# A second buffer for the high and low parts, taken from DMA scratch memory, the running logits sum on GpSimd, and new emission times

## The chip, the cores and the metric

The kernel runs on one core of one Trainium2 chip. The metric is device time in microseconds (us). The time before is the median of three runs, 523.21 us (522.85 to 523.69). One more execution was taken by the hardware profiler, and every duration in this document comes from it or from later profiles of the same kind.

Engine names follow the profile: PE is TensorE, PEld its weight loads, DVE is VectorE, ACT is ScalarE, POOL is GpSimd, SP is SyncE, whose queue issues most DMA transfers. L295 is line 295 of the kernel file.

## The reference

The reference computes attention over 4 batches, 8 heads, 768 positions and head size 64, in which a query sees only the keys whose 6-bit hash is the same as its own. The output feeds a soft mixture of experts.

```python
q_bits = (einsum(q, proj) > 0); k_bits = (einsum(k, proj) > 0)   # 6 bits each -> buckets
mask = q_bucket[:, :, :, None] == k_bucket[:, :, None, :]
scores = where(mask, scale * q @ k.T, -1e9)
attn = softmax(scores); x = attn @ v                      # then (4*768, 512)
logits = x @ phi                                          # 32 slots
d = softmax(logits, axis=0); slot_input = d.T @ x
slot_out[e] = relu(slot_input[e] @ w1[e]) @ w2[e]         # 8 experts, 4 slots each
out = softmax(logits, axis=1) @ slot_out
```

## The kernel before

There are 32 heads (4 batches of 8) and they are processed in pairs. For each pair one load brings `raw` (q and k of both heads, 2 x 128 x 768 floats). Because the fast matmul format of the kernel keeps fewer digits, q and k are split in a high and a low part: `split_hi` casts `raw` on ACT into parts 0 and 2 of the tile `w4` (L289, two casts), and `split_lo` writes raw minus high into parts 1 and 3 on DVE (L295, two operations; on POOL at L298 for the first pairs). `bits` makes the hash bits with eight matmuls (L332) and one DVE operation (`bt`, L325). Four kinds of DMA then spread rows of `w4` and `bt` over the operand tiles `XY` of each head: `spread_y`, `spread_l`, `spread_x`, `spread_bits`, all through line L302. `XY` has three buffers, `raw`, `w4` and `bt` one each.

For one head, `smax` (L375) multiplies into two PSUM buffers `smx`, and DVE takes row maxima of them (L378 and L381, nine reductions a head). `shift` turns the maxima into a row that `shift_rows` (L397 on PE, L400 on ACT, a DMA of `mr`) puts into `XY`. `scores` (L413) multiplies into three PSUM buffers `st`, and ACT takes the exponential into `pt` (L417). POOL adds the six blocks of `pt` into `acc` in five additions (L424 once, L430 four times), and `av` (L441, 24 matmul records) multiplies `pt` with `v`. `smax` of one head is interleaved with `scores` of the head before.

For a finished pair, `pair_sum`, `pair_turn` and `pair_rec` (L453, L489, L460) make reciprocals of the sums, `pair_x` (L504, L506) stores x, `pair_log` (L468) and `pair_add` make the pair's share of the logits: L480 multiplies, and L482 adds to the running sum `lacc` on DVE (not for the first pair of a batch). `batch_*` steps fold a batch into the slot softmax. After the last head the experts' layers run, with weights that `load_weights` has brought in during the attention.

The order of all this is written out by hand: each step has an emission time in the table `STEADY`, in slots relative to its pair (a pair is 12 slots, six a head), or in `ONCE`, in absolute slots. The steps are sorted by that time and emitted; an engine takes its instructions in exactly that order, and waits where the next one is not ready. The times only set the order; no step waits for a clock.

Of the kernel before, what the change touches and what calls it, by code (L numbers as in the profile page):

```python
# [42 lines left out]


STEADY = {
    ('acc', 0, 0): 0.91143595, ('acc', 0, 1): 3.17478349, ('acc', 0, 2): 3.59676867, ('acc', 1, 0): 10.88626624,
    ('acc', 1, 1): 11.33964379, ('acc', 1, 2): 11.82064114, ('av', 0, 0): 4.078226, ('av', 0, 1): 4.27318607,
    ('av', 0, 2): 4.47578804, ('av', 1, 0): 11.29101187, ('av', 1, 1): 11.30451101, ('av', 1, 2): 11.80872392,
    ('batch_both',): 20.1, ('batch_exp',): 23.0, ('batch_max',): 22.4, ('batch_scale',): 24.396,
    ('batch_share',): 27.6, ('batch_slots',): 26.173, ('batch_turn',): 23.9, ('batch_weigh',): 24.65,  # L50
    ('bits', 0): -13.95890534, ('load', 0): -21.84228255, ('load_v', 0): -1.51318162, ('load_v', 1): 4.63191299,
    ('pair_add', 0): 15.99028816, ('pair_log', 0): 15.89036858, ('pair_rec', 0, 0): 15.31234319,
    ('pair_rec', 0, 1): 15.74808174, ('pair_rec', 0, 2): 15.83774187, ('pair_sum', 0): 14.25462034,
    ('pair_turn', 0): 14.78228382, ('pair_x', 0, (0, 1)): 21.81002444, ('pair_x', 0, (2,)): 16.53595504,
    ('scores', 0, 0, 0): 0.42937858, ('scores', 0, 0, 1): 0.10975419, ('scores', 0, 1, 0): 0.37566801,
    ('scores', 0, 1, 1): 0.06354472, ('scores', 0, 2, 0): 2.73608952, ('scores', 0, 2, 1): 0.39545741,
    ('scores', 0, 3, 0): 1.17190303, ('scores', 0, 3, 1): 2.96375079, ('scores', 0, 4, 0): 0.91043595,
    ('scores', 0, 4, 1): 1.58215641, ('scores', 0, 5, 0): 2.32865234, ('scores', 0, 5, 1): 2.43752751,
    ('scores', 1, 0, 0): 6.82167698, ('scores', 1, 0, 1): 5.28419876, ('scores', 1, 1, 0): 5.49659969,
    ('scores', 1, 1, 1): 5.70056921, ('scores', 1, 2, 0): 9.5088345, ('scores', 1, 2, 1): 6.24519176,  # L60
    ('scores', 1, 3, 0): 6.27277748, ('scores', 1, 3, 1): 9.83928317, ('scores', 1, 4, 0): 9.71651955,
    ('scores', 1, 4, 1): 7.80253627, ('scores', 1, 5, 0): 9.44600188, ('scores', 1, 5, 1): 7.50325885,
    ('shift', 0): -2.89738435, ('shift', 1): 2.67478786, ('shift_rows', 0): -2.14833088,
    ('shift_rows', 1): 3.02147361, ('smax', 0, 0, 0): -7.00077299, ('smax', 0, 0, 1): -8.63468468,
    ('smax', 0, 1, 0): -8.20918051, ('smax', 0, 1, 1): -6.29379503, ('smax', 0, 2, 0): -5.39311908,
    ('smax', 0, 2, 1): -6.75745749, ('smax', 0, 3, 0): -6.47510133, ('smax', 0, 3, 1): -4.73315438,
    ('smax', 0, 4, 0): -8.59086819, ('smax', 0, 4, 1): -4.27385444, ('smax', 0, 5, 0): -4.25336427,
    ('smax', 0, 5, 1): -3.26636443, ('smax', 1, 0, 0): 2.40118286, ('smax', 1, 0, 1): -2.02963968,
    ('smax', 1, 1, 0): -2.01736929, ('smax', 1, 1, 1): 0.30153939, ('smax', 1, 2, 0): 0.03611274,
    ('smax', 1, 2, 1): 1.34851447, ('smax', 1, 3, 0): 1.74922724, ('smax', 1, 3, 1): 2.09633042,  # L70
    ('smax', 1, 4, 0): 2.28076515, ('smax', 1, 4, 1): -2.41700748, ('smax', 1, 5, 0): -2.06779907,
    ('smax', 1, 5, 1): 0.84522444, ('split_hi', 0): -14.12691859, ('split_lo', 0, 0): -13.3249754,
    ('split_lo', 0, 1): -13.04048452, ('spread_bits', 0): -13.92314133, ('spread_bits', 1): -8.21018051,
    ('spread_l', 0): -4.89960371, ('spread_l', 1): -6.85974162, ('spread_x', 0): -10.40239078,
    ('spread_x', 1): -7.05038, ('spread_y', 0): -11.52688803, ('spread_y', 1): -8.46779598,
}

ONCE = {
# [17 lines left out]
    ('one_turn', 31): 193.725, ('one_x', 30): 191.23, ('one_x', 31): 193.725, ('smax', 1, 0, 0): -2.3,  # L96
    ('smax', 1, 0, 1): -2.29, ('smax', 1, 1, 0): -2.28, ('smax', 1, 1, 1): -2.1, ('smax', 1, 2, 0): -2.05,
    ('smax', 1, 2, 1): -2.0, ('smax', 1, 3, 0): -1.99, ('smax', 1, 3, 1): -1.9, ('smax', 1, 4, 0): -1.8,
    ('smax', 1, 4, 1): 0.62, ('smax', 1, 5, 0): 0.63, ('smax', 1, 5, 1): 1.2, ('split_hi', 2): -1.5,
    ('split_lo', 2, 0): -1.45, ('split_lo', 2, 1): -1.44, ('spread_bits', 1): -7.869, ('spread_bits', 2): 0.4,  # L100
    ('spread_l', 0): -12.047, ('spread_l', 1): -12.02, ('spread_l', 2): 0.5, ('spread_x', 0): -12.04,
    ('spread_x', 1): -12.03, ('spread_x', 2): 0.6, ('spread_y', 1): -14.012, ('spread_y', 2): -1.2,
}


# [32 lines left out]
def lsh_attention_soft_moe(  # L138
# [141 lines left out]


    def split_hi(h):
        w = pp.tile([P, 4, S], F32R, name="w4", bufs=1)
# [4 lines left out]
        for x in range(2):
            nc.scalar.copy(w[:, 2 * x], st[h]["raw"][:, x])  # L289

    def split_lo(h, x):
        w = st[h]["w4"]
        raw = st[h]["raw"][:, x]
        if h > 2:
            nc.vector.scalar_tensor_tensor(out=w[:, 2 * x + 1], in0=raw, scalar=1.0, in1=w[:, 2 * x],  # L295
                                           op0=ALU.mult, op1=ALU.subtract)
# [175 lines left out]
    def pair_add(h):  # L472
        b, g = h // H, (h % H) // 2
        pt = st[h]["lp"]
        if g == 0:
# [4 lines left out]
        nc.vector.tensor_tensor(out=dst, in0=pt[:, 0:HC], in1=st[h]["rs"], op=ALU.mult)  # L480
        if g:
            nc.vector.scalar_tensor_tensor(out=lacc_of[b], in0=dst, scalar=1.0, in1=lacc_of[b],  # L482
                                           op0=ALU.mult, op1=ALU.add)
# [520 lines left out]
```

## Time and profile before

| | |
|---|---|
| median of three runs | 523.21 us |
| the profiled execution's own time | 524.37 us |
| its span, first to last instruction | 522.6 us |
| mean granted TensorE clock | 0.973 |
| PE busy | 482.3 us (92%) |
| DVE busy | 396.8 us (76%) |
| ACT busy | 245.6 us (47%) |
| POOL busy | 331.8 us (63%) |
| moved by DMA | 99.60 MB, mean 191 GB/s |

The span splits in a start (to about 31 us), the further pairs of heads, of some 27 us each, and the end (from about 452 us) with the experts' layers. Matmuls are pipelined, so busy time of PE is counted while any matmul is in flight; a gap of PE in the profile means that none was.

### The profile page before, as it was taken

To read this page: it belongs to the slowest core of one execution; us is meant where nothing else is said; L and a number is where in the kernel's file an instruction comes from. 1 tells how busy PE (TensorE), PEld (TensorE's weight loads), DVE (VectorE), ACT (ScalarE), POOL (GpSimd) and SP (SyncE) were. 2 spreads that over 40 slices of the span, in tenths; PEclk is the share of its full clock that TensorE was granted. 3 is DMA by queue.
4 is the path that set the end of the run, shared out by engine and by line. 5 is a ranking of instruction groups with operands and counts; after the bars stand their busy time and mean duration, and the time that the engine had idled before them with its cause. 6 is when DMAs were issued, how large, how long until landed. Compare 5 with 4: busy or idle time off the path is not lost.

```text
span 522.6 us, 9003 instructions
## 1 busy us (share of the span) xinstructions
PE 482.3 (92%) x3155; PEld 295.6 (57%) x3155; DVE 396.8 (76%) x700; ACT 245.6 (47%) x462; POOL 331.8 (63%) x226
## 2 busy tenths in 40 slices
PE   6889899999999999999999999999999999979992
PEld 4456565656565656565655656564656566453562
DVE  4735878989798989797998798989987967444333
ACT  4044546464555554545464636454745445412232
POOL 9258585868678776768587868586788687411200
PEclk9579999999999999999999999999999999989998
DMA  3757665666665557676656575757585676879977
GB/s 104 172 108 201 157 169 157 168 156 163 149 174 133 161 150 209 157 198 160 194 153 158 159 206 153 211 142 183 140 222 144 154 199 235 313 282 348 409 289 286
DMA packets 39802, 99.60 MB, mean 191 GB/s; under 512 B 7470, under 2 KB 13756, under 8 KB 39756
## 3 DMA queue, kind: packets, MB, share of 16 engines
q1 hardware_dynamic: 38956, 97.37, 64.9%
q10 hardware_dynamic: 608, 1.57, 1.4%
q8 instruction: 25, 0.41, 0.3%
q14 instruction: 21, 0.17, 0.1%
q0 software_dynamic: 192, 0.08, 0.1%
HBM read 52.76 MB, written 6.29 MB: 113 GB/s over the span
## 4 chain that ended last, share of the span: by engine, by line
PE 63%; DVE 14%; DMA 12%; SPq 5%; issue 3%; ACT 1%; DVEq 0%; ACTq 0%
PE st L413 17%; PE av L441 15%; PE smx L375 11%; DMA XY<-w 7%; DVE w L295 7%; SPq L302 5%; DMA XY<-bt 4%; PE qs L927 3%; PE qh L845 3%; PE av L243 2%; PE mi L468 2%; PE mi L453 2%; DVE mx L381 2%; PE mi L504 2%; DVE mx L378 2%
## 5 line engine op out<-in xcount | busy, mean ns | idle before, releaser
L430 POOL TENSOR_TENSOR acc<-acc,pt 128x768 f32<-128x768 f32 x125 | 239.8, 1919 | 72.0 <-ACT pt L417 64.5
L417 ACT ACTIVATE pt<-st 128x512 f32<-128x512 f32 x288 | 164.1, 597 | 66.3 <-PE st L413 55.9
L413 PE MATMUL st<-XY 128*128 128x512 f32 (+1 forms) x768 | 179.1, 347 | 2.3 <-DMA XY<-mr 2.3
L375 PE MATMUL smx<-XY 96*128 96x256 f32 (+1 forms) x384 | 127.4, 382 | 22.6 <-DVE mx L381 18.8
L381 DVE TENSOR_REDUCE mx<-smx 128x1 f32<-128x512 f32 x192 | 128.1, 680 | 15.8 <-PE smx L375 15.1
L413 PEld LDWEIGHTS st<-XY 128*128 128x128 f32 x768 | 127.7, 192 | 18.2 <-issue 4.2
L441 PE MATMUL av<-pt,v 128*64 128x384 f32 x768 | 130.9, 490 | 0.1
L375 PEld LDWEIGHTS smx<-XY 96*128 96x128 f32 x384 | 67.6, 194 | 59.5 <-DVE mx L381 30.4
L441 PEld LDWEIGHTS av<-pt,v 128*64 128x64 f32 x768 | 52.3, 137 | 76.0 <-issue 75.2
L424 POOL TENSOR_TENSOR acc<-pt 128x768 f32<-128x768 f32 x32 | 58.7, 1833 | 30.7 <-ACT pt L417 30.5
L295 DVE SCALAR_TENSOR_TENSOR w<-raw,w 128x768 fp32r<-128x768 f32 x28 | 60.3, 2192 | 22.8 <-ACT w L289 17.1
L378 DVE TENSOR_REDUCE mx<-smx 128x2 f32<-128x512 f32 x96 | 63.8, 678 | 13.2 <-PE smx L375 13.0
L445 ACT COPY avs<-av 128x384 f32<-128x384 f32 x32 | 15.3, 478 | 90.3 <-PE av L441 90.3
L289 ACT CAST w<-raw 128x768 fp32r<-128x768 f32 x32 | 25.0, 830 | 36.9 <-DMA XY<-w 14.8
L460 DVE RECIPROCAL sm<-sm 128x128 f32<-128x128 f32 x45 | 41.2, 919 | 0.0
L506 DVE TENSOR_TENSOR xq<-mi,r 128x256 f32<-128x256 f32 x45 | 17.6, 418 | 9.7 <-PE mi L504 9.7
L482 DVE SCALAR_TENSOR_TENSOR lacc<-sm,lacc 128x384 f32<-128x384 f32 x11 | 17.9, 1627 | 0.4
L504 PEld LDWEIGHTS mi<-ident,avs 128*128 128x128 f32 x90 | 10.4, 140 | 10.9 <-issue 9.0
L298 POOL TENSOR_TENSOR w<-raw,w 128x768 fp32r<-128x768 f32 x4 | 7.2, 1806 | 13.8 <-ACT w L289 13.8
L884 POOL CAST avs<-lacc 128x48 fp32r<-128x48 f32 x8 | 2.1, 265 | 21.5 <-ACT lacc L875 14.3
L504 PE MATMUL mi<-ident,avs 128*128 128x128 f32 x90 | 15.6, 282 | 0.0
L927 PE MATMUL qs<-w 128*32 128x256 f32 x232 | 15.2, 382 | 0.0
(169 smaller groups left out, 344.0 us busy)
## 6 DMA issues: line engine op xcount, KB each, us to landing
w<-w SPq DMA_DIRECT2D x61, 512.0 KB
XY<-w SPq DMA_DIRECT2D x61, 384.0 KB
raw<-qk SPq DMA_DIRECT2D x32, 384.0 KB
...
XY<-bt SPq DMA_DIRECT2D x62, 19.5 KB
```

Source lines behind the costliest of these rows:

```text
L295: nc.vector.scalar_tensor_tensor(out=w[:, 2 * x + 1], in0=raw, scalar=1.0, in1=w[:, 2 * x], op0=ALU.mult, op1=ALU.subtract)
L375: nc.tensor.matmul(pt[:, o:o + b - a], Ys[h % N_Y][0:96, 0, t * P:(t + 1) * P], Ys[h % N_Y][0:96, 1, a:b], start=True, stop=True)
L378: nc.vector.tensor_reduce(out=mx[:, n - 1:n + 1], in_=pt.rearrange("p (a x) -> p a x", a=2), axis=AX.X, op=ALU.max)
L381: nc.vector.reduce_max(out=mx[:, n:n + 1], in_=pt, axis=AX.X)
L413: nc.tensor.matmul(pt[:, o:o + b - a], x[:, 1, i * P:(i + 1) * P], x[:, 0, a:b], start=first, stop=not first)
L417: nc.scalar.activation(pts[i // 2][:, 512 * u:512 * u + 512], pt, AF.Exp, scale=D ** -0.5)
L424: nc.gpsimd.tensor_tensor(out=s["acc"], in0=pr[:, 0:S], in1=pr[:, S:2 * S], op=ALU.add)
L430: eng.tensor_tensor(out=s["acc"], in0=s["acc"], in1=pr[:, a * S:(a + 1) * S], op=ALU.add)
L441: nc.tensor.matmul(s["av"][64 * c:64 * c + 64, 0:HC], s["v"][:, i, :], pr[:, o + c * HC:o + (c + 1) * HC], start=(i == 0), stop=(i == NT - 1))
L460: nc.vector.reciprocal(out=rs[:, k * P:(k + 1) * P], in_=rs[:, k * P:(k + 1) * P])
L504: nc.tensor.transpose(pt[:, o:o + P], st[h + a]["avs"][:, k * P:(k + 1) * P], ident)
L927: nc.tensor.matmul(po[32 * j:32 * j + 32], hTs[g][:, f, 32 * j:32 * j + 32], wt[1, x, 2 * g + f // 4, j][:, (f % 4) * HM:(f % 4 + 1) * HM] ...
```

## The change

Four things are changed.

First, `w4` gets two buffers. A tile of it takes 4 x 768 x 4 = 12,288 bytes in each partition. The room comes from the memory that is set aside for transfer descriptors (`dynamic_dma_scratch_size=2048`).

Second, `split_lo` uses the plain subtraction instead of the operation with a scalar factor of 1.0, on the same engines as before.

Third, the addition to the running sum of the logits goes from DVE to POOL.

Fourth, the emission times are new: nearly all of `STEADY`, the times of the weight loads 5 to 16, and four single entries for one `scores` step of heads 3, 5, 7 and 9.

```diff
     def split_hi(h):
-        w = pp.tile([P, 4, S], F32R, name="w4", bufs=1)
+        w = pp.tile([P, 4, S], F32R, name="w4", bufs=2)
...
     def split_lo(h, x):
         w = st[h]["w4"]
-        raw = st[h]["raw"][:, x]
-        if h > 2:
-            nc.vector.scalar_tensor_tensor(out=w[:, 2 * x + 1], in0=raw, scalar=1.0, in1=w[:, 2 * x],
-                                           op0=ALU.mult, op1=ALU.subtract)
-        else:
-            nc.gpsimd.tensor_tensor(out=w[:, 2 * x + 1], in0=raw, in1=w[:, 2 * x], op=ALU.subtract)
+        eng = nc.vector if h > 2 else nc.gpsimd
+        eng.tensor_tensor(out=w[:, 2 * x + 1], in0=st[h]["raw"][:, x], in1=w[:, 2 * x], op=ALU.subtract)
...
         nc.vector.tensor_tensor(out=dst, in0=pt[:, 0:HC], in1=st[h]["rs"], op=ALU.mult)
         if g:
-            nc.vector.scalar_tensor_tensor(out=lacc_of[b], in0=dst, scalar=1.0, in1=lacc_of[b],
-                                           op0=ALU.mult, op1=ALU.add)
+            nc.gpsimd.tensor_tensor(out=lacc_of[b], in0=lacc_of[b], in1=dst, op=ALU.add)
...
-    ('bits', 0): -13.95890534, ('load', 0): -21.84228255, ('load_v', 0): -1.51318162, ('load_v', 1): 4.63191299,
+    ('bits', 0): -14.05014905, ('load', 0): -22.98001335, ('load_v', 0): -3.93842659, ('load_v', 1): -0.09675658,
...
-    nc = _bacc.Bacc("TRN2", target_bir_lowering=False, num_devices=1)
+    nc = _bacc.Bacc("TRN2", target_bir_lowering=False, num_devices=1, dynamic_dma_scratch_size=2048)
```

The new times move instructions on every engine. Two places are shown. The lines of the changed kernel are 2 to 3 lower or higher than those of before (L379 was L381, L296 was L295).

The first place is the split of a pair (here the fifth), on DVE. `xq` is `pair_x` of the pair before, `mx` are row maxima, `bt` the hash bits, `w` the low parts. Before:

```order
L506 TENSOR_TENSOR xq<-mi,r 128x2x2x64 x2
L378 TENSOR_REDUCE mx<-smx 128x2 x2
L325 TENSOR_SCALAR bt<-mi,con 128x384
L295 SCALAR_TENSOR_TENSOR w_1012<-raw,w_1012 128x768 x2
L381 TENSOR_REDUCE mx<-smx 128x1 x3
```

Now:

```order
L503 TENSOR_TENSOR xq<-mi,r 128x2x2x64 x2
L376 TENSOR_REDUCE mx<-smx 128x2 x2
L296 TENSOR_TENSOR w_1016<-raw,w_1016 128x768
L323 TENSOR_SCALAR bt<-mi,con 128x384
L296 TENSOR_TENSOR w_1016<-raw,w_1016 128x768
L379 TENSOR_REDUCE mx<-smx 128x1 x3
```

The first half of the split has moved ahead of the bits.

On PE the same place begins with the bits (`mi<-raw,pb`), goes on with the 24 matmuls of `av` (counted as 12 here), and then with `smax` of the pair's next head between `scores` of another. Before:

```order
L332 MATMUL mi<-raw,pb 32x384 x4
L441 MATMUL av<-pt_81,v_88 64x384 x4
L441 MATMUL av<-pt_82,v_88 64x384 x4
L441 MATMUL av<-pt_83,v_88 64x384 x4
L375 MATMUL smx<-XY_134 128x512
L413 MATMUL st<-XY_133 128x512 x2
L413 MATMUL st<-XY_133 128x256 x2
L375 MATMUL smx<-XY_134 128x512
L413 MATMUL st<-XY_133 128x256 x4
L413 MATMUL st<-XY_133 128x512 x2
L375 MATMUL smx<-XY_134 128x512
```

Now:

```order
L330 MATMUL mi<-raw,pb 32x384 x4
L439 MATMUL av<-pt_81,v_88 64x384 x4
L439 MATMUL av<-pt_82,v_88 64x384 x4
L439 MATMUL av<-pt_83,v_88 64x384 x4
L373 MATMUL smx<-XY_134 128x512
L411 MATMUL st<-XY_133 128x512 x2
L411 MATMUL st<-XY_133 128x256 x4
L373 MATMUL smx<-XY_134 128x512
L411 MATMUL st<-XY_133 128x512 x2
L411 MATMUL st<-XY_133 128x256 x2
L373 MATMUL smx<-XY_134 128x512
```

Between the first and the third `smax` matmul (`smx`) there stood ten `scores` matmuls (`st`), four of 512 columns and six of 256; the same ten stand there now, with the second `smax` two matmuls later. The third `smax` is as far from the end of `av` as before.

The second place is the queue of SP around the spreading of the bits (`XY<-bt`) of a pair's even head. Before:

```order
L302 DMA XY_135<-mr 1x12x128
L302 DMA XY_134<-bt 13x384 x2
L302 DMA XY_134<-bt 12x384 x2
L180 DMA w<-w 128x1024
L279 DMA v_87<-vt 128x384
L302 DMA XY_134<-w_2145 64x2x768 x2
```

Now:

```order
L300 DMA XY_135<-mr 1x12x128
L300 DMA XY_134<-w_2147 64x2x768
L300 DMA XY_134<-w_2147 32x2x768
L281 DMA v_88<-vt 128x384
L300 DMA XY_134<-bt 13x384 x2
L300 DMA XY_134<-bt 12x384 x2
```

The bits of the even head stood right behind the row `mr` of another head. They now stand behind two copies out of `w4` (the high parts for `smax`, then 32 rows of low and high parts) and behind a load of `v` for an odd head. The buffer `v_88` is the one that `av` at the first place reads, so the load waits for the end of that `av`.

More of the change, by code (lines that the diff above doesn't have):

```diff
@@ L45 @@
 STEADY = {
-    ('acc', 0, 0): 0.91143595, ('acc', 0, 1): 3.17478349, ('acc', 0, 2): 3.59676867, ('acc', 1, 0): 10.88626624,
-    ('acc', 1, 1): 11.33964379, ('acc', 1, 2): 11.82064114, ('av', 0, 0): 4.078226, ('av', 0, 1): 4.27318607,
-    ('av', 0, 2): 4.47578804, ('av', 1, 0): 11.29101187, ('av', 1, 1): 11.30451101, ('av', 1, 2): 11.80872392,
+    ('acc', 0, 0): 3.32219408, ('acc', 0, 1): 3.51642133, ('acc', 0, 2): 4.07952489, ('acc', 1, 0): 8.00580368,
+    ('acc', 1, 1): 10.50985253, ('acc', 1, 2): 11.62567304, ('av', 0, 0): 4.52736825, ('av', 0, 1): 4.52836825,
@@ L53 @@
[L53 to L73, printed above, removed]
@@ L74 @@
-    ('spread_l', 0): -4.89960371, ('spread_l', 1): -6.85974162, ('spread_x', 0): -10.40239078,
-    ('spread_x', 1): -7.05038, ('spread_y', 0): -11.52688803, ('spread_y', 1): -8.46779598,
+    ('bits', 0): -14.05014905, ('load', 0): -22.98001335, ('load_v', 0): -3.93842659, ('load_v', 1): -0.09675658,
+    ('pair_add', 0): 16.08052489, ('pair_log', 0): 16.01386709, ('pair_rec', 0, 0): 15.38551575,
+    ('pair_rec', 0, 1): 15.52428406, ('pair_rec', 0, 2): 15.23093309, ('pair_sum', 0): 14.27844673,
@@ new lines @@
+    ('scores', 1, 0, 0): 4.84785546, ('scores', 1, 0, 1): 5.76179514, ('scores', 1, 1, 0): 5.78130163,
+    ('scores', 1, 1, 1): 7.11688462, ('scores', 1, 2, 0): 9.09032258, ('scores', 1, 2, 1): 4.86037114,
+    ('scores', 1, 3, 0): 5.83602334, ('scores', 1, 3, 1): 7.96283788, ('scores', 1, 4, 0): 9.54442858,
+    ('scores', 1, 4, 1): 8.16841547, ('scores', 1, 5, 0): 9.27892106, ('scores', 1, 5, 1): 9.79855832,
+    ('shift', 0): -3.25513296, ('shift', 1): 3.03750886, ('shift_rows', 0): -2.41358372,
@@ new lines @@
+    ('shift_rows', 1): 3.69484621, ('smax', 0, 0, 0): -4.98693151, ('smax', 0, 0, 1): -8.53163395,
+    ('smax', 0, 1, 0): -8.47671594, ('smax', 0, 1, 1): -7.21677346, ('smax', 0, 2, 0): -3.68506512,
+    ('smax', 0, 2, 1): -7.20355182, ('smax', 0, 3, 0): -7.16664801, ('smax', 0, 3, 1): -8.47172351,
+    ('smax', 0, 4, 0): -6.71159669, ('smax', 0, 4, 1): -4.42464018, ('smax', 0, 5, 0): -4.38260211,
+    ('smax', 0, 5, 1): -6.21344464, ('smax', 1, 0, 0): 2.12519565, ('smax', 1, 0, 1): -2.64113359,
@@ new lines @@
+    ('smax', 1, 1, 0): -2.42174694, ('smax', 1, 1, 1): -0.44479647, ('smax', 1, 2, 0): 2.41023163,
+    ('smax', 1, 2, 1): 0.99477885, ('smax', 1, 3, 0): 0.99577885, ('smax', 1, 3, 1): 2.69509412,
+    ('smax', 1, 4, 0): 0.32890374, ('smax', 1, 4, 1): -2.4938082, ('smax', 1, 5, 0): -2.45339367,
+    ('smax', 1, 5, 1): 0.61962065, ('split_hi', 0): -14.38602349, ('split_lo', 0, 0): -14.20531537,
+    ('split_lo', 0, 1): -13.47847782, ('spread_bits', 0): -12.09280343, ('spread_bits', 1): -7.7834394,
@@ L76 @@
+    ('spread_l', 0): -12.17922931, ('spread_l', 1): -8.60318625, ('spread_x', 0): -8.82285848,
+    ('spread_x', 1): -7.49145173, ('spread_y', 0): -13.22782847, ('spread_y', 1): -7.9636022,
 }
@@ L95 @@
     ('one_rec', 31): 193.725, ('one_sum', 30): 189.395, ('one_sum', 31): 193.725, ('one_turn', 30): 189.777,
[L96 to L102, printed above, removed]
+    ('one_turn', 31): 193.725, ('one_x', 30): 191.23, ('one_x', 31): 193.725, ('scores', 3, 2, 0): 20.38221043,
+    ('scores', 5, 2, 0): 32.38221043, ('scores', 7, 2, 0): 44.38221043, ('scores', 9, 2, 0): 56.38221043,
+    ('smax', 1, 0, 0): -2.3, ('smax', 1, 0, 1): -2.29, ('smax', 1, 1, 0): -2.28, ('smax', 1, 1, 1): -2.1,
+    ('smax', 1, 2, 0): -2.05, ('smax', 1, 2, 1): -2.0, ('smax', 1, 3, 0): -1.99, ('smax', 1, 3, 1): -1.9,
+    ('smax', 1, 4, 0): -1.8, ('smax', 1, 4, 1): 0.62, ('smax', 1, 5, 0): 0.63, ('smax', 1, 5, 1): 1.2,
+    ('split_hi', 2): -1.5, ('split_lo', 2, 0): -1.45, ('split_lo', 2, 1): -1.44, ('spread_bits', 1): -7.869,
+    ('spread_bits', 2): 0.4, ('spread_l', 0): -12.047, ('spread_l', 1): -12.02, ('spread_l', 2): 0.5,
+    ('spread_x', 0): -12.04, ('spread_x', 1): -12.03, ('spread_x', 2): 0.6, ('spread_y', 1): -14.012,
+    ('spread_y', 2): -1.2,
 }
```

17 lines of the change are left out of this document (11 added, 6 removed).

## The prediction

> **What bounds the kernel now.** I read the page first, its busy times:
>
> ```profile
> PE 482.3 (92%) x3155; PEld 295.6 (57%) x3155; DVE 396.8 (76%) x700; ACT 245.6 (47%) x462; POOL 331.8 (63%) x226
> ```
>
> PE is all but full, so the question is what PE waits for. The second view is the list of waits, cut to the attention's steady stretch (40 to 430 us); its columns are total, times, longest:
>
> ```profile
> PE smx L375 <- DVE mx L381: 16.6, 14, 1.6
> PE mi L637 <- ACT dl L616: 0.3, 1, 0.3
> ```
>
> There is one wait of size: some 1.3 us once a pair, before a `smax` matmul whose PSUM buffer DVE has not yet reduced. Third, the timeline around one of them (start, length, engine and line, count, idle before and its releaser). The first row is from SP's own timeline, the last two from narrower windows, which show one instruction of a merged row:
>
> ```profile
> 205.40 4.42 SPq L302 DMA_DIRECT2D XY<-w  x4
> 210.07 8.15 POOL L430 TENSOR_TENSOR acc<-acc,pt 128x768 f32<-128x768 f32 x4 [0.51 <-ACT pt L417]
> 210.99 1.29 DVE L378 TENSOR_REDUCE mx<-smx 128x2 f32<-128x512 f32 x2
> 211.15 0.85 PE L332 MATMUL mi<-raw,pb 128*32 128x384 f32 x8
> 211.31 0.24 ACT L400 CAST mr<-mi 12x128 fp32r<-12x128 f32 x1
> 211.93 4.09 PE L441 MATMUL av<-pt,v 128*64 128x384 f32 x24
> 212.19 0.67 DVE L325 TENSOR_SCALAR bt<-mi,con 128x384 fp32r<-128x384 f32 x1
> 212.89 3.19 SPq L302 DMA_DIRECT2D XY<-bt  x4
> 213.63 1.57 ACT L289 CAST w<-raw 128x768 fp32r<-128x768 f32 x2 [2.09 <-DMA XY<-mr]
> 214.50 4.54 DVE L295 SCALAR_TENSOR_TENSOR w<-raw,w 128x768 fp32r<-128x768 f32 x2 [1.64 <-ACT w L289]
> 215.95 0.50 PE L375 MATMUL smx<-XY 96*128 96x512 f32 x1
> 218.97 1.96 DVE L381 TENSOR_REDUCE mx<-smx 128x1 f32<-128x512 f32 x3
> 219.70 0.50 PE L375 MATMUL smx<-XY 96*128 96x512 f32 x1 [1.30 <-DVE mx L381]
> 213.87 1.83 POOL L430 TENSOR_TENSOR acc<-acc,pt 128x768 f32<-128x768 f32 x1
> 214.50 2.02 DVE L295 SCALAR_TENSOR_TENSOR w<-raw,w 128x768 fp32r<-128x768 f32 x1 [1.64 <-ACT w L289]
> ```
>
> The story runs backwards. PE's third `smax` after `av` waits at 219.70 for a reduction that DVE could only begin at 218.97, because the two halves of the split held DVE until 219.04. They began at 214.50, after 1.64 us of waiting for ACT's casts, and these began 2.09 us late. The row names the copy of `mr`, but a cast into the only `w4` has to wait for the copies out of the old `w4`: the four XY<-w copies, whose issue ended at 209.82 and which land later.
>
> The halves are also long for another reason:
>
> ```profile
> L295 DVE SCALAR_TENSOR_TENSOR w<-raw,w x28: 945/2342/2601, 53.8 to 405.1; 128x768 fp32r<-128x768 f32 x28
> L430 DVE TENSOR_TENSOR acc<-acc,pt 128x768 f32<-128x768 f32 x2 | 1.9, 950 | 0.0
> ```
>
> 945 ns at best, 2342 in the median. The first half started at 214.50 while POOL's addition ran to 213.87 + 1.83 = 215.70, and ended 0.82 after that: it stood still until POOL was done. The Trainium skill says this as a rule (SBUF — State Buffer, Who interferes with whom): a DVE instruction with two SBUF inputs and a GpSimd instruction that reads SBUF exclude each other, and the later one waits for the whole of the other. The trace agrees with it here, to 0.01 us or so.
>
> **The trace holds one pair without the late cast.** It is the one after 373 us, where a batch was folded:
>
> ```profile
> 373.17 0.53 PE L332 MATMUL mi<-raw,pb 128*32 128x384 f32 x4
> 374.26 1.57 ACT L289 CAST w<-raw 128x768 fp32r<-128x768 f32 x2 [0.68 <-issue]
> 375.79 3.49 DVE L295 SCALAR_TENSOR_TENSOR w<-raw,w 128x768 fp32r<-128x768 f32 x2
> 378.28 0.48 PE L375 MATMUL smx<-XY 96*128 96x512 f32 x1
> 380.55 0.40 PE L375 MATMUL smx<-XY 96*128 96x512 f32 x1
> 399.82 0.53 PE L332 MATMUL mi<-raw,pb 128*32 128x384 f32 x4
> 264.58 0.53 PE L332 MATMUL mi<-raw,pb 128*32 128x384 f32 x4
> 292.95 0.53 PE L332 MATMUL mi<-raw,pb 128*32 128x384 f32 x4
> ```
>
> The casts begin 1.09 us after the bits instead of 2.48 (213.63 - 211.15), and PE has no wait: the third `smax` comes 2.27 us after the first, instead of 219.70 - 215.95 = 3.75. So the wait costs 1.48 us of start to start, a little more than the 1.30 in which no matmul was in flight. From bits to bits this pair takes 26.65 us, the other batch pair shown 28.37: 1.72 apart.
>
> **The change part by part.** *Second buffer of w4.* The casts now wait for copies of two pairs ago, long landed. They can follow the cast of `mr`, 211.31 + 0.24 = 211.55, and the first, half of 1.57, is through at 212.35. DVE ends its reductions at 212.28. So the first half can start at 212.4 instead of 214.50, 2.1 us sooner. To be free of PE's wait, DVE must have reduced the first buffer (0.65, a third of 1.96) by 215.95 + 2.27 = 218.22, so both halves must be over by 217.57. At worst each half meets an addition of POOL that has just begun: 212.4 + 2 x (1.83 + 0.82) = 217.7, and 0.1 to 0.2 us of wait are left. The bits' 0.67 us, which now stand between the halves, lie inside the second POOL addition, which starts when the first half lets go. At best there is no addition in the way: 212.4 + 2 x 0.95 + 0.67 = 215.0. I take 0.1 us left on average, by the worse end, since POOL has five additions close together here.
>
> Worth of the wait: 16.6 us are 13 times 1.30, so 13 pairs, and each is worth 1.30 (gap only) to 1.72 (batch pairs). I take 1.5, near the 1.48: 13 x 1.5 = 19.5 us, bounds 16.6 and 22.
>
> *Plain subtraction.* 950 ns in the L430 row on DVE, also two SBUF inputs and 768 elements, against 945: nothing.
>
> *Running sum on POOL.*
>
> ```profile
> L482 DVE SCALAR_TENSOR_TENSOR lacc<-sm,lacc x11: 942/1662/2011, 94.1 to 441.2; 128x384 f32<-128x384 f32 x11
> L600 POOL TENSOR_TENSOR dl<-lacc,dl 64x384 f32<-64x384 f32 x3 | 3.0, 1006 | 9.2 <-ACT dl L599 9.2
> L480 DVE TENSOR_TENSOR sm<-mi,sm 128x384 f32<-128x384 f32 x11 | 6.1, 558 | 1.1
> 211.14:237.88 26.74, 25.44 (x157) 15.80 (x157) 23.60 (x38) 13.72 (x26) 19.05 (x11) 1.00 0.67 179
> 225.05 7.72 POOL L430 TENSOR_TENSOR acc<-acc,pt 128x768 f32<-128x768 f32 x4 [4.07 <-ACT pt L417]
> 228.81 0.56 DVE L480 TENSOR_TENSOR sm<-mi,sm 128x384 f32<-128x384 f32 x1
> 234.45 1.83 POOL L424 TENSOR_TENSOR acc<-pt 128x768 f32<-128x768 f32 x1 [1.68 <-ACT pt L417]
> ```
>
> DVE loses 1.66 us in 11 pairs, POOL gains about 1.0 (384 elements per partition, as L600). The fourth row is one pair: its length, then busy time of PE, PEld, DVE, ACT and POOL. POOL has 26.74 - 19.05 = 7.7 us free in a pair, and its queue puts the sum after the five additions of the even head: they end at 225.05 + 7.72 = 232.8, the multiplication that the sum waits for (L480) at 229.4, and POOL then idles 1.68 us for exponentials, which cover the 1.0. If that cover were gone, it would cost up to 1.0 x 11 = 11 us. DVE's 1.66 lie beside the `av` of the even head, where PE does not wait for them: no gain counted. The Trainium skill advises against such a move (GPSIMD Engine Reference, Engine selection: two-input elementwise work is about twice as slow on GpSimd as on VectorE). By that page the addition would take an estimated 1.1 us on POOL, twice L480's 0.56, and the move would lose; the rows show 1006 ns there and 1662 on DVE, so the trace speaks the other way in this place, and the sum is the same by both.
>
> *New times.* TensorE gets the same matmuls. At the start the first bits move ahead of ten warming matmuls:
>
> ```profile
> 7.68 0.81 PE L332 MATMUL mi<-raw,pb 128*32 128x384 f32 x5
> 11.52 0.71 PE L375 MATMUL smx<-XY 96*128 96x256 f32 x3 [3.03 <-DVE XY L325]
> ```
>
> These may fill part of the 3.03 us: 0 to 1.2 us gained, I take 0.5. The last exponential of the odd head now stands behind the casts on ACT, 1.57 us later at most, and the third of `av` that needs it begins 2.7 us into the 4.09: no cost. The weights' loads are needed only after 452 us: nothing. The spreading of the bits behind a load of `v` is a rival, below. What is late next is DVE's pace, 23.60 of 26.74 busy; without the 1.66 and with less blocking it is some 22 of 25.2, so still behind PE.
>
> *Sum.* The profiled execution's own time is 524.37, its span 522.6. 524.4 - 19.5 + 13 x 0.1 - 0.5 = 505.7; the median of the runs stands 1.16 below it: 504.5. I say 505. About 0.2% (1 us) is what a measurement here can tell from no change.
>
> **The rivals.** *The wait half stays.* The halves are caught twice and the casts start later than I read, by 0.5 us or so: 13 x 0.6 left, 512. For it: POOL's five additions leave few openings. Against it: 212.4 counts every row of before at its full length. Chance 0.15.
>
> *Another wait takes its place.* With the gap gone, DVE's reductions or POOL's additions (19.05 + 1.0 of 25.2, behind which `pair_sum` and the exponentials stand) set the pair: 1.0 to 1.5 us a pair is given back, 13 to 19 us, so 518 to 524. Against it: PE waited for nothing in the pair after 373 us. Chance 0.08, a half of it no change.
>
> *Slower.* SP's queue runs in order, and the bits of the even head now stand behind the load of `v`, which waits for the end of `av` (216.02). The rows give the load's issue, a copy's issue to landing, and where the next head's first `smax` stands:
>
> ```profile
> 216.69 0.42 SPq L279 DMA_DIRECT2D v<-vt  x1
> 214.59 1.86 DMA XY<-bt
> 225.16 0.47 PE smx L375 x3
> ```
>
> Issue ends at 216.02 + 0.42 + 3.19 = 219.6, the last copy (issued 0.8 before that) lands by some 220.7, and `smax` stands at 225.16 - 1.5 = 223.7 without the gap: 3 us to spare. Copies that land later than that make PE wait; beyond 4.5 the gain is gone. Behind two weight pieces of 512 KB, now issued together, at the pair's 179 GB/s (5.9 us), 5.9 - 4.5 = 1.4 us a pair would be lost, 18 us: 541. Against it: those pieces are issued some 7 us earlier. Chance 0.06. That the second buffer does not reach the casts would leave 523; the casts then show the same late start. Chance 0.01.
>
> **How the numbers follow.** Forecast 0.70 (501 to 509), half the wait 0.15, another wait 0.08, slower 0.06, no effect 0.01. The range reaches from 501 (the larger worth, 523.2 - 22) to 515, and so takes in the second case. Faster: 0.70 + 0.15 + 0.04 = 0.89; same 0.04; slower 0.07.
>
> **What would show it.** Right: no wait of PE on DVE at `smax` in the list of waits, or under 2 us of 16.6; casts that begin within 1.2 us of the bits; first half of the split before the bits' `bt`, over about 6 us after the bits' start; bits to bits 25.2 us in a plain pair; the running sum on POOL near 1.0 us and no one waiting for it. Wrong: pairs still above 26 us, or a DMA named as PE's releaser at `smax`.

## The result, and the profile after

The kernel after takes 503.28 us in the median of four runs (502.43 to 503.86), beside 523.4 us for the kernel before (522.85 to 523.69, four runs): a ratio of 0.9615, with a 95% interval of 0.9596 to 0.9635. The forecast was 505 in a range of 501 to 515. The profiled execution took 502.74 us with a span of 501.0, at a mean granted clock of 0.971.

The busy times first. DVE has lost 28 us, POOL gained 17, and PE is now 95% busy in a shorter span:

```profile
PE 476.5 (95%) x3155; PEld 295.5 (59%) x3155; DVE 368.8 (74%) x689; ACT 242.5 (48%) x462; POOL 348.5 (70%) x237
```

The list of waits, PE's own rows in the attention's steady stretch (40 to 410 us here). Where 14 waits on DVE at `smax` stood with 16.6 us, there is one of 0.2. A new one has come, on the copies of `mr`:

```profile
PE st L411 <- DMA XY<-mr: 2.6, 5, 0.8
...
PE smx L373 <- DVE mx L379: 0.2, 1, 0.2
```

The timeline of the same place in a pair as was shown of before (the lines are two lower, the split is L296 now):

```profile
200.22 1.56 ACT L291 CAST w<-raw 128x768 fp32r<-128x768 f32 x2
...
200.29 0.85 PE L330 MATMUL mi<-raw,pb 128*32 128x384 f32 x8
...
201.07 4.09 PE L439 MATMUL av<-pt,v 128*64 128x384 f32 x24
201.07 0.96 DVE L296 TENSOR_TENSOR w<-raw,w 128x768 fp32r<-128x768 f32 x1
...
201.95 0.67 DVE L323 TENSOR_SCALAR bt<-mi,con 128x384 fp32r<-128x384 f32 x1
...
202.54 1.99 DVE L296 TENSOR_TENSOR w<-raw,w 128x768 fp32r<-128x768 f32 x1
...
205.63 0.69 DVE L379 TENSOR_REDUCE mx<-smx 128x1 f32<-128x512 f32 x1 [1.10 <-PE smx L373]
```

The casts (ACT L291) begin 0.07 us before the bits (PE L330), not 2.5 after them. The first half of the split runs at 0.8 us after the bits' start, unhindered at 0.96 us. The second ends at 204.53, 4.2 us after the bits' start; before, both were over after 7.9. The last row turns the old picture round: DVE waits 1.10 us for PE's `smax`, and no longer PE for DVE.

Length and busy times of this pair (PE, PEld, DVE, ACT, POOL), then the split and the running sum in the list of groups:

```profile
200.29:225.27 24.98, 24.98 (x157) 15.84 (x156) 20.47 (x37) 13.39 (x26) 20.68 (x12) 1.00 0.67 172
```

```profile
L296 DVE TENSOR_TENSOR w<-raw,w 128x768 fp32r<-128x768 f32 x28 | 50.3, 1797 | 0.6
...
L480 POOL TENSOR_TENSOR lacc<-lacc,sm 128x384 f32<-128x384 f32 x11 | 11.1, 1010 | 0.0
```

A pair takes 24.98 us from bits to bits where it took 26.74, and PE is busy in all of it. DVE's idle time ahead of its halves of the split, the last number of its row, is 0.6 us.

Where the 21.6 us of span came from is read from the first bits matmul of a pair. These are the third and the last pair of before and, in the second fence, of after:

```profile
48.48 0.84 PE L332 MATMUL mi<-raw,pb 128*32 128x384 f32 x6
...
399.82 0.85 PE L332 MATMUL mi<-raw,pb 128*32 128x384 f32 x8
```

```profile
46.20 0.85 PE L330 MATMUL mi<-raw,pb 128*32 128x384 f32 x8
...
379.87 0.85 PE L330 MATMUL mi<-raw,pb 128*32 128x384 f32 x8
```

Up to the third pair 48.48 - 46.20 = 2.3 us were won. The pairs between gave (399.82 - 48.48) - (379.87 - 46.20) = 17.7. The rest, (522.6 - 399.82) - (501.0 - 379.87) = 1.65, lies behind the last pair's bits, where before had one more wait of PE on DVE (1.29 us at 408.37).

### The profile page after: what moved, and what is told of

The parts are those of the page before. It is cut to its first block, busy times and chain, and to the rows that moved or that the text cites. A ratio compares the mean times of both kernels' runs of the same rounds, so it can differ in the third digit from the quotient of the medians.

```text
span 501.0 us, 8993 instructions
## 1 busy us (share of the span) xinstructions
PE 476.5 (95%) x3155; PEld 295.5 (59%) x3155; DVE 368.8 (74%) x689; ACT 242.5 (48%) x462; POOL 348.5 (70%) x237
## 4 chain that ended last, share of the span: by engine, by line
PE 84%; DMA 9%; DVE 2%; SPq 1%; ACT 1%; issue 1%; POOL 0%; ACTq 0%; DVEq 0%
PE st L411 28%; PE av L439 21%; PE smx L373 14%; DMA XY<-mr 8%; PE qs L924 3%; PE qh L842 3%; PE mi L451 2%; PE mi L330 2%; PE mi L501 2%; DMA raw<-qk 2%; PE mi L466 1%; PE av L245 1%; PE mi L486 1%; SPq L300 1%; PE mi L651 1%; PE qa L887 1%
## 5 line engine op out<-in xcount | busy, mean ns | idle before, releaser
L428 POOL TENSOR_TENSOR acc<-acc,pt 128x768 f32<-128x768 f32 x125 | 245.9, 1967 | 30.0 <-ACT pt L415 21.5
L415 ACT ACTIVATE pt<-st 128x512 f32<-128x512 f32 x288 | 162.1, 596 | 62.3 <-PE st L411 57.7
L411 PE MATMUL st<-XY 128*128 128x256 f32 (+1 forms) x768 | 176.2, 346 | 4.7 <-DMA XY<-mr 4.5
L379 DVE TENSOR_REDUCE mx<-smx 128x1 f32<-128x512 f32 x192 | 129.8, 684 | 61.2 <-PE smx L373 58.9
L411 PEld LDWEIGHTS st<-XY 128*128 128x128 f32 x768 | 129.9, 192 | 23.9 <-DMA XY<-mr 4.0
L373 PE MATMUL smx<-XY 96*128 96x256 f32 (+1 forms) x384 | 121.9, 374 | 4.1 <-DVE mx L379 3.2
L296 DVE TENSOR_TENSOR w<-raw,w 128x768 fp32r<-128x768 f32 x28 | 50.3, 1797 | 0.6
L291 ACT CAST w<-raw 128x768 fp32r<-128x768 f32 x32 | 25.0, 827 | 0.2
L330 PE MATMUL mi<-raw,pb 128*32 128x384 f32 x128 | 15.1, 520 | 0.5 <-DMA raw<-qk 0.5
L842 PE MATMUL qh<-w,siT 128*32 128x512 f32 x128 | 14.6, 595 | 0.0
L398 ACT CAST mr<-mi 12x128 fp32r<-12x128 f32 x32 | 7.9, 245 | 13.2 <-DMA XY<-w 13.2
```

The lines of the kernel that those rows point to most:

```text
L296: eng.tensor_tensor(out=w[:, 2 * x + 1], in0=st[h]["raw"][:, x], in1=w[:, 2 * x], op=ALU.subtract)
L373: nc.tensor.matmul(pt[:, o:o + b - a], Ys[h % N_Y][0:96, 0, t * P:(t + 1) * P], Ys[h % N_Y][0:96, 1, a:b], start=True, stop=True)
L379: nc.vector.reduce_max(out=mx[:, n:n + 1], in_=pt, axis=AX.X)
L411: nc.tensor.matmul(pt[:, o:o + b - a], x[:, 1, i * P:(i + 1) * P], x[:, 0, a:b], start=first, stop=not first)
L415: nc.scalar.activation(pts[i // 2][:, 512 * u:512 * u + 512], pt, AF.Exp, scale=D ** -0.5)
L428: eng.tensor_tensor(out=s["acc"], in0=s["acc"], in1=pr[:, a * S:(a + 1) * S], op=ALU.add)
```

## The experiments

The theory: the single `w4` made the casts late, the late casts made the split late, and the split held the row maxima for which PE waited. The first rival: the new emission times did it, and the buffer is not needed. The second: the running sum that left DVE did it. Ratios are to runs of the kernel before on the same chip, with 95% intervals.

**The second buffer alone**, with the room that it needs, in the kernel before:

```diff
-        w = pp.tile([P, 4, S], F32R, name="w4", bufs=1)
+        w = pp.tile([P, 4, S], F32R, name="w4", bufs=2)
...
-    nc = _bacc.Bacc("TRN2", target_bir_lowering=False, num_devices=1)
+    nc = _bacc.Bacc("TRN2", target_bir_lowering=False, num_devices=1, dynamic_dma_scratch_size=2048)
```

> The kernel before with the second buffer of w4 alone (and the smaller descriptor memory that makes room); old emission times, old split, running sum on VectorE. Theory (the wait of 1.3 us a pair comes from casts that wait for copies out of the only w4): the casts follow the cast of mr within 1 us of the bits, both halves of the split are over 6.1 us after the bits' start, TensorE's 16.6 us of waits on VectorE at smax fall below 3 us, and the time is 504 to 507 us. Rival (the new order of the split and of the matmuls is what removes the wait): the waits stay above 10 us and the time above 515 us.

505.66 us, ratio 0.9646 (0.9589 to 0.9702). PE's only wait left in the steady stretch, and a pair with its casts:

```profile
PE st L413 <- DMA XY<-mr: 0.8, 1, 0.8
```

```profile
202.35 0.85 PE L332 MATMUL mi<-raw,pb 128*32 128x384 f32 x8
...
202.66 1.56 ACT L289 CAST w<-raw 128x768 fp32r<-128x768 f32 x2
...
203.98 4.33 DVE L295 SCALAR_TENSOR_TENSOR w<-raw,w 128x768 fp32r<-128x768 f32 x2
```

```profile
202.35:227.51 25.16, 25.16 (x156) 15.84 (x156) 23.31 (x38) 13.60 (x26) 19.66 (x11) 1.00 0.72 194
```

The casts follow 0.31 us behind the bits, the split is over 6.0 us behind them, and the pair has 25.16 us with PE busy throughout. From the third to the last pair's bits there are 382.53 - 49.74 = 332.8 us, beside 351.3 before and 333.7 after:

```profile
49.74 0.85 PE L332 MATMUL mi<-raw,pb 128*32 128x384 f32 x8
...
382.53 0.85 PE L332 MATMUL mi<-raw,pb 128*32 128x384 f32 x8
```

So the buffer by itself is enough for the wait and for all that the pairs gained. (The smaller descriptor memory goes with it here and in all kernels that follow with two buffers; no run changes that memory by itself.)

**The new times with one buffer**: the kernel after with `bufs=1`.

```diff
-        w = pp.tile([P, 4, S], F32R, name="w4", bufs=2)
+        w = pp.tile([P, 4, S], F32R, name="w4", bufs=1)
```

> The changed kernel with one buffer of w4 again, all else new. Theory in its plain form (the second buffer is needed): the casts start 2 us after the bits again, the wait of 1.3 to 1.5 us a pair is back, 520 to 523 us. Rival (the new times alone empty w4 early enough, since the last copies out of it are now issued some 4 us before the next casts): casts at most 1 us late, waits below 5 us in total, 503 to 508 us.

505.68 us, ratio 0.9658 (0.9598 to 0.9719). Here the rival held. But for the batch pairs, most pairs have 24.97 to 25.5 us (one 25.75), and only the first of the steady stretch, with 27.7, shows the old chain:

```profile
47.76 0.85 PE L330 MATMUL mi<-raw,pb 128*32 128x384 f32 x8
...
50.34 1.56 ACT L291 CAST w<-raw 128x768 fp32r<-128x768 f32 x2 [2.56 <-DMA XY<-w]
...
56.43 0.50 PE L373 MATMUL smx<-XY 96*128 96x512 f32 x1 [0.81 <-DVE mx L379]
```

The casts wait for the copies out of `w4` (this time the row names them) and are 2.6 us late. This kernel has the smaller descriptor memory as well, so that memory alone does not cure the wait. Later the copies are early enough. In this kernel, SP's queue has the last copies out of `w4` ahead of the bits at 125.88 here:

```profile
119.57 1.43 SPq L300 DMA_DIRECT2D XY<-w  x2
```

They are issued by 121.0, 4.9 us ahead of those bits; before, issue ended at 209.82, only 1.3 us ahead of the bits at 211.15. So buffer and times are two cures for one wait: each alone gives about 0.965, and together they give 0.9615, not the sum. The three intervals overlap, so that both together beat one of them is not shown.

**The running sum, both ways**: back on DVE in the kernel after, and alone on POOL in the kernel before.

```diff
-            nc.gpsimd.tensor_tensor(out=lacc_of[b], in0=lacc_of[b], in1=dst, op=ALU.add)
+            nc.vector.scalar_tensor_tensor(out=lacc_of[b], in0=dst, scalar=1.0, in1=lacc_of[b],
+                                           op0=ALU.mult, op1=ALU.add)
```

> The changed kernel with the running sum on VectorE again (the operation with a factor of 1.0), all else new. Theory (the sum lies beside the av of the even head, where nothing waits): 502.5 to 504.5 us, no change that can be told; VectorE busy 18 us more, GpSimd 11 us less. Rival (taking it off VectorE is a part of the gain): 505 us or more, with new waits of TensorE at smax after the even head's av.

505.44 us, ratio 0.9649 (0.9594 to 0.9704). The sum costs DVE 1983 ns each now, in the mean; the second view is a pair of this kernel (its length, then busy time of PE, PEld, DVE, ACT and POOL):

```profile
L480 DVE SCALAR_TENSOR_TENSOR lacc<-sm,lacc 128x384 f32<-128x384 f32 x11 | 21.8, 1983 | 0.4
```

```profile
199.31:224.69 25.38, 25.13 (x156) 15.84 (x156) 22.60 (x38) 13.33 (x26) 19.91 (x11) 1.00 0.66 163
```

```profile
PE smx L373 <- DVE mx L379: 1.0, 4, 0.3
```

The waits at `smax` come to 1.0 us, 0.8 more than after. In that pair the sum runs from 215.67 to 217.88, the reduction behind it is late, and PE waits 0.25 us for it after the even head's `av`. Five of the last six pairs without a batch have 25.37 or 25.38 us where the kernel after has 24.97 in a pair without a wait. That is what the expectation's rival described, with its time (505 or more); some 5 x 0.4 = 2 us by these rows. Waits on `mr` are in this run too (3.8 us, the longest 1.8), a kind that the kernel after has without the sum on DVE. In the medians the run can't be told from the kernel after, since the intervals overlap.

```diff
-            nc.vector.scalar_tensor_tensor(out=lacc_of[b], in0=dst, scalar=1.0, in1=lacc_of[b],
-                                           op0=ALU.mult, op1=ALU.add)
+            nc.gpsimd.tensor_tensor(out=lacc_of[b], in0=lacc_of[b], in1=dst, op=ALU.add)
```

> The kernel before with the running sum on GpSimd alone. Theory: VectorE does 18 us less, none of it on the path, 522 to 524 us. Rival (the relief of VectorE or of the shared port counts by itself): 520 us or less. If GpSimd's queue were tight, it would be slower: 525 us or more.

521.71 us, ratio 0.9964 (0.9935 to 0.9993): 1.9 us at best estimate. PE's waits on DVE go from 16.6 us in 14 to

```profile
PE smx L375 <- DVE mx L381: 14.7, 12, 1.4
```

The second rival is out as the main cause, since twelve of the fourteen waits stand. The two that are gone are one of 0.20 us and the one of 1.29 behind the last pair's bits; that one is also missing in a run below whose sum is on DVE (13 waits, 15.4 us), so it can't be put to the sum. Plain pairs have 26.6 us for 26.7. The Trainium skill's advice for such an addition (GPSIMD Engine Reference, Engine selection) is VectorE, since two-input work is about twice as slow on GpSimd. In this place the rows say the reverse, 1010 ns on POOL against 1983 on DVE, where the operation has to wait for POOL's own additions: the one at 215.67 starts 0.01 us behind such an addition and takes 2.21 us. The least of the eleven on DVE took 659 ns, so it is the waiting that turns the choice round.

**The kernel after once more**, unchanged, as the measure for the two runs of the start and the first move of the load, all on one chip.

> The kernel after, unchanged, beside its own variants on one chip: 503.3 us, plain pairs 24.98 us, five waits of PE on the copies of mr with 2.6 us in all. It is the measure for the other runs of this group.

501.37 us, ratio 0.9581 (0.9532 to 0.963). This profile has one wait on `mr` where the first had five:

```profile
PE st L411 <- DMA XY<-mr: 1.8, 1, 1.8
```

So these waits vary from execution to execution, and 2 us between runs of this kernel mean little (its six runs here lie between 500.34 and 507.81).

**The start, both ways**: the warming matmuls ahead of the first bits again in the kernel after, and ten of them behind the bits in the kernel before.

```diff
-    ('first_y', 1): -20.551, ('first_y', 2): -3.524, ('keep_warm', 'a'): -14.0, ('keep_warm', 'b'): -2.6,
+    ('first_y', 1): -20.551, ('first_y', 2): -3.524, ('keep_warm', 'a'): -14.06, ('keep_warm', 'b'): -2.6,
```

> The kernel after with the warming matmuls put back ahead of the first bits, by one emission time. Theory: of what the new times gave beyond the wait, 2.3 us came at the start, since the first bits run at 4.4 us instead of 7.5 and the whole of the first pair with them. Then the first smax stands again near 11.5 us instead of 8.25 and the time is 2 to 3 us above that of the kernel after. Rival, as predicted: only 0 to 1.2 us of the start hang on it, since the first smax waits for loads and copies; then 0.5 us or less is lost.

503.83 us, ratio 0.9631 (0.9574 to 0.9688). Bits and first `smax` are late, and the old gap of 3.03 us is back:

```profile
6.80 0.52 PE L330 MATMUL mi<-raw,pb 128*32 128x384 f32 x3
...
10.85 0.71 PE L373 MATMUL smx<-XY 96*128 96x256 f32 x3 [3.03 <-DVE XY L323]
```

```diff
-    ('first_y', 1): -20.551, ('first_y', 2): -3.524, ('keep_warm', 'a'): -14.0, ('keep_warm', 'b'): -2.6,
+    ('first_y', 1): -20.551, ('first_y', 2): -3.524, ('keep_warm', 'a'): -13.95, ('keep_warm', 'b'): -2.6,
```

> The kernel before with the first bits moved ahead of ten of the warming matmuls, by one emission time, nothing else. Theory: the start alone gives 2 to 3 us, so the time is 521 to 522 where the kernel before has 523.4 to 524.1, and the waits at smax stay at 16 us. Rival: the casts of the first pairs and the copies set the start, and the time stays within 0.5 us of the kernel before.

522.08 us, ratio 0.9966 (0.9941 to 0.999), and the waits at `smax` stay (13 with 15.4 us).

```profile
4.48 1.64 PE L332 MATMUL mi<-raw,pb 128*32 128x384 f32 x6
...
5.97 2.02 PE L243 MATMUL av<-pt,ones 128*32 128x128 f32 x17
8.57 0.71 PE L375 MATMUL smx<-XY 96*128 96x256 f32 x3 [0.58 <-DVE XY L325]
...
46.25 0.95 PE L332 MATMUL mi<-raw,pb 128*32 128x384 f32 x8
```

The third pair's bits start at 46.25 instead of 48.48, 2.2 us sooner; by the ratio the move is worth 0.5 to 3.1 us. That point moves from profile to profile: with the same old start it lay at 47.94 in the run with the sum on POOL. So the move gives 1.7 to 2.2 us in the kernel before. In the other direction the medians differ by 2.5 us on the same chip, with overlapping intervals, but in the profile only 0.9 us are left at the third pair's bits, at 47.09 against 46.20. Other kernels with the new start have this point between 45.55 (the sum on DVE) and 46.90 (the split's old operation), so in this direction a gain isn't shown.

**The split's old operation** in the kernel after.

```diff
-        eng = nc.vector if h > 2 else nc.gpsimd
-        eng.tensor_tensor(out=w[:, 2 * x + 1], in0=st[h]["raw"][:, x], in1=w[:, 2 * x], op=ALU.subtract)
+        raw = st[h]["raw"][:, x]
+        if h > 2:
+            nc.vector.scalar_tensor_tensor(out=w[:, 2 * x + 1], in0=raw, scalar=1.0, in1=w[:, 2 * x],
+                                           op0=ALU.mult, op1=ALU.subtract)
+        else:
+            nc.gpsimd.tensor_tensor(out=w[:, 2 * x + 1], in0=raw, in1=w[:, 2 * x], op=ALU.subtract)
```

> The kernel after with the old three-operand form of the split (multiply by 1.0, then subtract) in place of the plain subtraction. Theory, as predicted: both forms read two SBUF inputs of 768 elements and cost the same, so the halves of the split keep their 0.95 us at best and some 1.8 us in the mean, and the time is that of the kernel after within 0.2%. Rival: the plain form is shorter or holds POOL less; then the mean of a half rises from 1.80 towards the 2.19 us of before, and the time by 1 us or more.

503.51 us, ratio 0.9615 (0.9582 to 0.9648), the kernel after's own ratio.

```profile
L297 DVE SCALAR_TENSOR_TENSOR w<-raw,w 128x768 fp32r<-128x768 f32 x28 | 52.1, 1861 | 0.5
```

1861 ns in the mean for 1797: nothing that shows in the time.

**The new wait on `mr`.** In the kernel after the load of the next `raw` stands ahead of the odd head's copies on SP's queue. These are PE's wait, SP's queue, and the copy of `mr` in the chain of waits (issue to landing):

```profile
115.94 0.97 PE L411 MATMUL st<-XY 128*128 128x512 f32 x4 [0.75 <-DMA XY<-mr]
```

```profile
105.56 0.93 SPq L193 DMA_DIRECT2D raw<-qk  x2
106.54 3.37 SPq L300 DMA_DIRECT2D XY<-w  x3
110.03 0.92 SPq L300 DMA_DIRECT2D XY<-mr  x1
```

```profile
110.03 5.87 DMA XY<-mr
```

The load was ahead of that copy in the kernel before, too:

```profile
194.63 2.85 SPq L191 DMA_DIRECT2D raw<-qk  x2
199.16 0.82 SPq L302 DMA_DIRECT2D XY<-mr  x1
```

So the load's place alone does not make the wait new, and why PE comes to wait for `mr` only now isn't shown; with the buffer alone it did so once (0.8 us). A copy of 6 KB lands 5.87 us after its issue. To see whether the 768 KB of `raw` ahead of it do that, the load was moved behind it, first too far:

```diff
-    ('bits', 0): -14.05014905, ('load', 0): -22.98001335, ('load_v', 0): -3.93842659, ('load_v', 1): -0.09675658,
+    ('bits', 0): -14.05014905, ('load', 0): -19.45, ('load_v', 0): -3.93842659, ('load_v', 1): -0.09675658,
```

> The kernel after with one emission time changed: the load of the next raw piece (two packets of 384 KB) goes to SP's queue behind the copies of mr of the odd head, instead of ahead of the w and mr copies. Theory: the copies of mr land late (0.75 us of wait at 115.9 us) because that load is ahead of them in the queue. Then the 2.6 us of waits of PE on mr at st go to under 0.5, and the time is 2 to 3 us below that of the kernel after: some 500.7 us; the raw piece is needed 17 us after its issue now and still lands in time. Rival: mr is late because of the w copies ahead of it, one of which waits; then the waits stay at 2 to 3 us and the time is the same to 0.5 us. Second rival: the later load is itself late, and the casts of the next pair start later than 1 us after the bits; then the time is equal or longer.

519.49 us, ratio 0.9907 (0.9871 to 0.9943). The expectation's last rival struck, and at a size it did not name:

```profile
123.35 2.19 SPq L193 DMA_DIRECT2D raw<-qk  x2
...
128.28 1.75 ACT L291 CAST w<-raw 128x768 fp32r<-128x768 f32 x2 [0.91 <-DMA raw<-qk]
```

The load is behind the copies of that head's bits too, which wait for DVE; it is issued 5.0 us ahead of the next bits instead of 17.6, and bits and casts wait together for it. On one chip the move costs 519.49 - 501.37 = 18.1 us of a gain of 22, which tells how far one issue on an in-order queue reaches. Next, directly behind `mr`:

```diff
-    ('bits', 0): -14.05014905, ('load', 0): -22.98001335, ('load_v', 0): -3.93842659, ('load_v', 1): -0.09675658,
+    ('bits', 0): -14.05014905, ('load', 0): -20.0, ('load_v', 0): -3.93842659, ('load_v', 1): -0.09675658,
```

> The kernel after with the load of the raw piece put directly behind the copy of mr of the odd head in SP's queue, past the three w copies and that copy and no further; the run before, which put it behind all of that head's copies, left it 5 us for 17 and paid 18 us. Theory: now it is issued some 13 us ahead of the bits, in time, and the copies of mr no longer stand behind its 768 KB: PE's waits on mr between 40 and 410 us, 2.6 us in one profile of the kernel after and 1.8 in another, go under 0.5, and the time is 1 to 3 us below the kernel after (ratio to the kernel before about 0.955). Rival: the waits on mr come from the w copies and the load of the weights around it, and stay at 2 to 3 us, with the time unchanged. Second rival: the load now lands beside the bt copies, and these come late for smax: a DMA is then named before smax and the time is longer.

508.17 us, ratio 0.9718 (0.9683 to 0.9754). No wait of PE on `mr` is left, but the second rival came true in the early pairs:

```profile
112.28 1.68 SPq L193 DMA_DIRECT2D raw<-qk  x2
...
114.71 4.12 SPq L300 DMA_DIRECT2D XY<-bt  x4
```

```profile
122.97 0.35 PE L373 MATMUL smx<-XY 96*128 96x256 f32 x1 [2.15 <-DMA XY<-bt]
```

The copies of `bt` now stand behind the load, and `smax` waits for them in three places, 4.3 us in all, between 72 and 180 us. Later pairs had no wait, so the last try moves the load only from the ninth pair on:

```diff
+    ('load', 16): 76.0, ('load', 18): 88.0, ('load', 20): 100.0, ('load', 22): 112.0, ('load', 24): 124.0, ('load', 26): 136.0, ('load', 28): 148.0, ('load', 30): 160.0,
```

> The kernel after with the load of the raw piece directly behind the odd head's copy of mr, but only from the ninth pair on (h = 16 and later); the early pairs keep their order. In the run that moved it in all pairs the waits on mr were gone and the pairs from 180 us on had 24.97 us, with 26.6 in the last batch pair, where the kernel after had 27.3 to 30.6 in four profiles; only the pairs from 72 to 180 us lost, with copies of bt landing late beside the loads of the weights. Theory: here the early pairs are those of the kernel after, the last batch pair is 26.6 us, no PE wait on mr is left after 180 us, and the time is some 1 to 2.5 us below that of the kernel after (501 to 502 where that has 503.3; the ratio to the kernel before 0.957 to 0.959). Rival: the wait on mr in the last batch pair does not come from the load ahead of it in the queue; then that pair stays above 27.3 us and the time is the same.

501.55 us, ratio 0.9587 (0.9555 to 0.962). Below are all waits of PE between 40 and 410 us, the queue in the last batch pair, and that pair as a whole, in this kernel; the last row is the same pair of the kernel after, from its repeated run.

```profile
PE smx L374 <- DVE mx L380: 0.2, 1, 0.2
```

```profile
365.14 0.83 SPq L301 DMA_DIRECT2D XY<-mr  x1
366.02 0.96 SPq L194 DMA_DIRECT2D raw<-qk  x2
```

```profile
350.42:377.00 26.58, 26.58 (x177) 16.74 (x177) 22.76 (x45) 15.09 (x32) 21.84 (x15) 1.00 0.70 194
```

```profile
349.48:377.97 28.49, 26.73 (x175) 16.71 (x175) 22.75 (x45) 15.07 (x32) 21.80 (x15) 1.00 0.66 169
```

The wait is gone and that pair is 1.9 us shorter. With the load behind `mr` in all pairs it had 26.59 us, while every kernel above with two buffers and the load ahead of `mr` had 27.3 us or more there. So in that pair the wait does not come without the load ahead of `mr`. Its profiled span of 497.9 us is the shortest of all. Against the kernel before it is 4.1% faster, but its interval overlaps with both of the kernel after's, so that it beats the kernel after is not shown.

**The order of `smax` on PE by itself**: the second buffer in the kernel before, with the `smax`, `shift` and `shift_rows` times of the kernel after (28 numbers of the table; two of them):

```diff
-    ('shift_rows', 1): 3.02147361, ('smax', 0, 0, 0): -7.00077299, ('smax', 0, 0, 1): -8.63468468,
+    ('shift_rows', 1): 3.69484621, ('smax', 0, 0, 0): -4.98693151, ('smax', 0, 0, 1): -8.53163395,
```

> The kernel before with the second buffer, and the emission times of smax, shift and shift_rows of the kernel after, all else in the order of before. It asks whether the order of the same smax matmuls on PE is worth time by itself. Theory: the kernel after had 24.98 us in a plain pair and the second buffer alone 25.17, because groups of smax matmuls of 256 and 512 columns issue faster in the new order; then plain pairs are 25.0 here and the smax matmuls of the pairs take 0.3 us less from start to start. Rival: the 0.2 us a pair comes from the other moves (scores, av, or the sum that left DVE); then plain pairs stay at 25.15 to 25.2 us.

562.54 us, ratio 1.0743 (1.0706 to 1.078). It did not answer its question: a pair of some 28.75 us holds new waits that drown it.

```profile
207.47 1.81 POOL L430 TENSOR_TENSOR acc<-acc,pt 128x768 f32<-128x768 f32 x1 [2.45 <-ACT pt L417]
207.55 1.75 DVE L388 SCALAR_TENSOR_TENSOR mz<-m,bigs 128x6 f32<-128x6 f32 x1
```

```profile
209.56 0.33 PE L397 MATMUL mi<-ident,mz 128*128 128x128 f32 x1 [1.60 <-DVE mz L390]
```

An operation on six elements a partition takes 1.75 us instead of its usual 0.17, because it starts 0.08 us behind an addition of POOL, and PE stands 1.60 us for it; the list of waits from 40 to 430 us has 13 such waits with 20.8 us in all. The rule that the prediction named (the Trainium skill, SBUF — State Buffer, Who interferes with whom) agrees: POOL ends at 209.28, DVE 0.02 us later at 209.30. So an operation that is short alone can take as long as the addition beside which it starts.

## Why the prediction was right

**The late cast** was the cause, as told. The second buffer alone removes all 14 waits, and its pair of 25.16 us is the 25.2 that was forecast. The casts start 0.31 us behind the bits there and 0.07 ahead of them in the kernel after, and the halves are over by 6.0 us, and by 4.2 in the pair shown: the steps that the prediction gave as signs all came, but for the first half, which with the buffer alone still stands behind `bt`.

**The size.** 13 waits at 1.5, less 0.1 each left over, made 18.2 us. The buffer alone, to which this sum belongs, gave 351.3 - 332.8 = 18.5 between the third and the last pair's bits, where twelve of these waits stood: 1.5 each, and none of them left over. For the whole change the pairs and the end gave 17.7 + 1.65 = 19.3, and that agreement is in part luck, since two misses nearly cancel. The waits on `mr` at `st`, 2.6 us in the profile after, were not foreseen: another wait did take the place, as a rival had it, but not at the 13 us and more of that rival. And a pair has 24.98 us with the new times, not 25.2. PE idles neither in this pair nor in that with the buffer alone (25.16), and the matmuls are the same ones, so "TensorE gets the same matmuls" was too simple: in another order they are through 0.18 us sooner. Which of them gain isn't shown. PE's busy time by tile falls from 7.67 to 7.43 us (`smx`), from 11.18 to 10.86 (`st`) and from 4.63 to 4.50 (`mi`), 0.69 in all, but a moment in which matmuls of two tiles are in flight counts for both. The experiment meant to isolate the order of `smax` failed, so why the order matters stays open.

**The start** was the mis-sized term: 0.5 taken, 0 to 1.2 as bounds, 2.3 measured between the two kernels, and 1.7 to 2.2 for the move by itself in the kernel before. The ten warming matmuls that the bits passed stand in the trace as twenty records, 3 + 17 behind the bits, and the 17 alone take 2.02 us (the row of 5.97 above). Of the gap of 3.03 us all but 0.58 closed; 1.2 would have been ten records.

**Plain subtraction**: nothing, as said (0.9615 on both sides). **Running sum**: 1010 ns on POOL beside the forecast 1.0, and PE's list of waits names it nowhere. "No gain counted" was a little too low: in the kernel after, the sum on DVE would reach beyond the `av` beside which it was thought to lie and make a late pair 0.4 us longer. In the kernel before, the move is worth 0.4 to 3.4 us (the interval of the ratio, times 524), and how it gains them isn't shown. The 1 us that the prediction took as what can be told from no change is too little for such runs, whose intervals are 0.25% to 0.6% to each side. **The bits behind the load of `v`** made no one wait in the profile after. The mechanism of that rival is real, but the load to fear was that of `raw`: where a run put the copies of `bt` behind it, they did come late. **The lock between DVE and POOL** is as the prediction has it, but "0.01 us or so" does not come out of its rows: the half ends 0.82 us behind POOL's addition, and the shortest half takes 0.945, so rule and rows agree to 0.13 us.

**What the prediction gave wrongly to one part:** it put the whole of the gain on the second buffer. The run with one buffer shows the new times to be a nearly full substitute.
